# A fused mLSTM-and-experts kernel: a PSUM tile for each bank, another order of the attention step, and the division of the rows moved to GpSimd

## The chip, the cores and the metric

The kernel runs on one core of a Trainium2 chip. The metric is the device time of one execution in microseconds (us), the median of several. The engines are TensorE (PE in the profile; its weight loads are PEld), VectorE (DVE), ScalarE (ACT), GpSimd (POOL) and SyncE (SP), which here only starts transfers; transfers by a list of indices are started by POOL.

## What is computed

An mLSTM (attention with a running matrix state, 4 batches, 8 heads, 768 tokens, head size 40) and behind it a mixture of eight experts, of which each token takes the best one. The attention's rows, 3072 tokens by 320, are the experts' input.

```python
for t in range(S):                                    # attention, per batch and head
    m_new = np.maximum(f_gate[:, :, t] + m, i_gate[:, :, t])
    f_stab, i_stab = np.exp(f_gate[:, :, t] + m - m_new), np.exp(i_gate[:, :, t] - m_new)
    C = f_stab * C + i_stab * outer(v_t, k_t)
    n = f_stab * n + i_stab * k_t
    denom = np.maximum(np.abs(n @ q_t), 1.0)
    y[:, :, t] = sigmoid(o_gate[:, :, t]) * (C @ q_t) / denom
logits = x @ w_gate                                   # x: y as (3072, 320) rows
expert_idx, gate_w = argmax(logits), softmax(logits)[argmax]
for e in range(8):
    mask = expert_idx == e
    out[mask] = gate_w[mask, None] * (np.maximum(x[mask] @ w1[e], 0.0) @ w2[e])
```

## The kernel before

**Attention.** 24 items (128 tokens of one batch, all heads) pass through a pipeline in program order; nothing reorders it, each engine runs its own instructions in the order written. `step(s)` does for item s the `scores` (PE) and `pmul` (DVE, the masked product pp), for item s+1 `weigh` (POOL: qg, kw, cd), for item s-2 `natural` (PE, L322: yT is brought to token-major form in the bank x_ps, with the denominators and the gate logits in further columns) and then, woven together, `state(s-2)` (DVE writes the state cz), `finish(s-2)` (DVE: reciprocal r of the denominators, the divided rows xs at L339, the logits lg), `routing` of a group of items, and some of the long gate operations (`gates`). Then come `choose` when a group of 4 or 2 items is complete (DVE: d, the one-hot oh, running sums ohs), and only behind it, at the step's end, `attend(s-1)` (PE, L290 to L299: the state's and the tokens' products into h_ps) and `gated(s-1)` (DVE, yT). `spread` and `decay` (PE, ACT, POOL) prepare item s+2. `store` writes xs to x_dram in HBM. `scatter` (POOL) writes each token's number to the list of its expert; `place`, `count` and `total` work out its slot with small matmuls (L391 to L393, L431) and DVE operations, the last of them a cast to integer (L413).

**Experts.** `take` loads an expert's list, and `gather` (POOL, L513) fetches J tiles of T rows each by it. `transpose_x` (PE, ACT, DVE) turns them into columns, split into a high part xh and a low part xl; `third(k)` does a third of that. `first` makes eight groups of products with w1 (L546), each group in one of three PSUM banks, and ACT and DVE make the high part hh (L555) and the low part hl (L556) from each. `second` multiplies by w2 (L569) for one tile of tokens at a time, in one of two banks, ACT scales (L573) and POOL scatters y to the output (L574). The heaviest expert, 0, is done in parts "a" (256 tokens, taken early) and "b" (the rest). Expert r+1 is taken at the start of expert r and transposed inside `second` of it. The experts have J x T of 4x128 (three), 4x112, 3x128 (two) and 3x112 (two) rows.

The banks are assigned by these lines; bc_ps and h_ps are one tile of two banks each, and the program tracks a PSUM tile as a whole:

```python
bc_ps = ps1.tile([P, 2, 512], F32, name="bc_ps")
g_ps = ps1.tile([P, 512], F32, name="g_ps")
h_ps = ps1.tile([P, 2, 512], F32, name="h_ps")
bank = [*s_ps, bc_ps[:, 0], bc_ps[:, 1], g_ps, h_ps[:, 0], h_ps[:, 1], x_ps]
turn = {n: itertools.cycle(t) for n, t in (("xt", [*bank[:2], bank[7]]), ("ph", bank[2:5]), ("py", bank[5:7]))}
```

## Time and profile before

| | |
|---|---|
| median of 3 runs | 462.13 us (461.16 to 467.69) |
| the profiled execution | 459.98 us, span of its trace 458.3 us |
| mean granted TensorE clock | 0.907 |
| busy share | PE 80%, DVE 54%, ACT 39%, POOL 35% |
| attention, to the first expert's products | 0 to 182.97 us |
| expert 0, while the other lists are made | 182.97 to 229.87 us |
| experts 1 to 7 | 229.87 to 445.81 us |

A time is the start of an instruction in microseconds from the span's start. Busy time is the time in which an engine worked; idle time is put down to what ended it. The granted clock is the share of full speed that the throttle left to TensorE in a stretch.

### The profile page before, as it was taken

The numbers are of one execution on the slowest core, as the hardware profiler recorded it, in microseconds if no ns is written. First come the engines' busy times: TensorE is split into PE (matmuls) and PEld (weight loads), VectorE is DVE, ScalarE is ACT, GpSimd is POOL, SyncE is SP. The second block draws the span as 40 slices with busy tenths as digits, with TensorE's granted clock in tenths as the row PEclk, the third lists the DMA queues.
The fourth block names the chain that finished last, engine by engine and source line by source line (L and its number), as shares of the span: only waits on it lengthen the run. The fifth ranks groups of instructions, "written<-read, shape, count | busy, mean of one in ns | idle before, by whom it ended". The sixth has DMA issues, their size and how long they took to land. (4 is left out here: it accounts for less than half of the span.)

```text
span 458.3 us, 8799 instructions
## 1 busy us (share of the span) xinstructions
PE 367.6 (80%) x3250; PEld 326.3 (71%) x3250; DVE 248.2 (54%) x587; ACT 179.0 (39%) x429; POOL 162.4 (35%) x198
## 2 busy tenths in 40 slices
PE   7496598786978879679888987988988978889870
PEld 3485487676767768578867875877887868889770
DVE  4779666768698897545335325426515435263200
ACT  4544235354456460145234323424425334353210
POOL 2555258575685653334040240131130140222010
...
GB/s 223 213 264 170 143 119 209 152 187 173 192 245 267 190 50 103 139 81 211 91 91 65 165 105 59 133 119 95 136 122 87 169 130 117 145 126 35 2 20 12
DMA packets 33599, 61.37 MB, mean 134 GB/s; under 512 B 8724, under 2 KB 20253, under 8 KB 33538
## 3 DMA queue, kind: packets, MB, share of 16 engines
...
q14 instruction: 19, 0.16, 0.2%
q10 hardware_dynamic: 192, 0.18, 0.1%
...
## 5 line engine op out<-in xcount | busy, mean ns | idle before, releaser
L225 ACT ACTIVATE dd<-bc_ps,aT 128x128 f32<-128x128 f32 x192 | 52.1, 382 | 84.2 <-PE bc_ps L207 59.5
L574 POOL DMA_INDIRECT out<-y,ls x24 | 23.6, 981 | 160.4 <-ACT y L573 153.4
L569 PE MATMUL h_ps<-w2h,hh 128*128 128x320 f32 (+1 forms) x224 | 72.0, 321 | 8.4 <-ACT y L573 7.2
L569 PE MATMUL h_ps<-w2l,hh 128*128 128x320 f32 (+1 forms) x224 | 69.5, 310 | 0.0
L569 PE MATMUL h_ps<-w2h,hl 128*128 128x320 f32 (+1 forms) x224 | 69.4, 310 | 0.0
L546 PE MATMUL bc_ps<-xh,w1h 128*128 128x512 f32 (+4 forms) x129 | 48.5, 378 | 25.3 <-DVE hl L556 24.0
L556 DVE SCALAR_TENSOR_TENSOR hl<-bc_ps,hh 128x256 fp32r<-128x256 f32 (+4 forms) x48 | 26.5, 552 | 68.4 <-ACT hh L555 67.3
L569 PEld LDWEIGHTS h_ps<-w2h,hh 128*128 128x128 f32 (+1 forms) x224 | 41.3, 184 | 13.2 <-ACT y L573 11.4
L546 PEld LDWEIGHTS bc_ps<-xh,w1h 128*128 128x128 f32 x129 | 25.5, 198 | 33.7 <-DVE hl L556 29.6
L555 ACT ACTIVATE hh<-bc_ps 128x256 fp32r<-128x256 f32 (+4 forms) x48 | 23.4, 489 | 65.9 <-PE bc_ps L546 61.5
L546 PE MATMUL bc_ps<-xh,w1l 128*128 128x512 f32 (+4 forms) x129 | 45.6, 355 | 0.0
L322 PE MATMUL x_ps<-cs,yT 105*128 105x98 f32 x184 | 31.0, 320 | 15.4 <-DVE yT L307 15.4
L271 DVE TENSOR_TENSOR pp<-s_ps,dd 128x512 f32<-128x512 f32 x48 | 31.0, 685 | 21.9 <-PE s_ps L265 13.0
L232 POOL TENSOR_SCALAR_AFFINE_SELECT dd<-dd 128x1024 f32<-128x1024 f32 (+1 forms) x25 | 26.6, 1065 | 42.8 <-ACT dd L225 37.5
L569 PEld LDWEIGHTS h_ps<-w2l,hh 128*128 128x128 f32 (+1 forms) x224 | 41.3, 184 | 0.0
L569 PEld LDWEIGHTS h_ps<-w2h,hl 128*128 128x128 f32 (+1 forms) x224 | 41.3, 184 | 0.0
L322 PEld LDWEIGHTS x_ps<-cs,yT 105*128 105x128 f32 x184 | 26.7, 223 | 19.0 <-DVE yT L307 17.1
L573 ACT ACTIVATE y<-h_ps,ls 128x320 f32<-128x320 f32 (+1 forms) x24 | 12.7, 527 | 68.1 <-issue 55.0
L496 DVE TENSOR_TENSOR w1l<-raw,w1h 128x1024 fp32r<-128x1024 f32 x24 | 31.5, 1315 | 6.6 <-ACT w1h L492 6.6
L295 PE MATMUL h_ps<-pp,tk 128*41 128x128 f32 x368 | 33.2, 337 | 0.9 <-DVE cz L316 0.6
L513 POOL DMA_INDIRECT xg<-x_dram,ls x26 | 27.7, 1066 | 14.5 <-issue 5.5
L496 DVE TENSOR_TENSOR w2l<-raw,w2h 128x640 fp32r<-128x640 f32 x32 | 26.0, 822 | 12.5 <-ACT w2h L492 11.7
...
## 6 DMA issues: line engine op xcount, KB each, us to landing
...
xg<-x_dram,ls POOLq DMA_INDIRECT x26
```

The source lines that it names most:

```text
L225: nc.scalar.activation(dd[:, h, :], bc_ps[:, h // 4, (h % 4) * P : (h % 4 + 1) * P], AF.Exp, bias=aT[:, c, i : i + 1], scale=-1.0,)
L232: nc.gpsimd.affine_select(part, part, pattern=[[0, n], [1, P]], compare_op=ALU.is_ge, fill=0.0, base=0, channel_multiplier=-1)
L271: nc.vector.tensor_mul(pp[:, 4 * k : 4 * k + 4], s_ps[k].rearrange("p (h t) -> p h t", t=P), t["dd"][:, 4 * k : 4 * k + 4])
L295: nc.tensor.matmul(out_of(it, h), v[:, h], t["pp"][:, h], start=c == 0, stop=True, skip_group_check=True)
L322: nc.tensor.matmul(x[:, o], t["yT"][:, o * P : (o + 1) * P], cs[:OR, C_R + o * XW : C_R + (o + 1) * XW], start=True, stop=True,)
L496: nc.vector.tensor_sub(w[name + "l"][:, c], t, f32(w[name + "h"][:, c]))
L513: nc.gpsimd.indirect_dma_start(out=xg[:T, j], out_offset=None, in_=x_dram[: 1 + items * P], in_offset=bass.IndirectOffsetOnAxis(ap=ls[:T, ...
L546: nc.tensor.matmul(ph[:, :n], a[:, k, fs], b[:, k, :n], start=not last and i == 0, stop=last and i == 2)
L555: nc.scalar.activation(hh[:, f, :n], ph[f][:, :n], AF.Relu)
L556: nc.vector.scalar_tensor_tensor(hl[:, f, :n], ph[f][:, :n], 0.0, f32(hh[:, f, :n]), ALU.max, ALU.subtract)
L569: nc.tensor.matmul(py[:T], a[:, f, ts], b[:, f], start=(f == 0 and i == 0), stop=(f == NF - 1 and i == 2))
L574: nc.gpsimd.indirect_dma_start(out=out, out_offset=bass.IndirectOffsetOnAxis(ap=ls[:T, j, 1:2].bitcast(I32), axis=0), in_=y[:T], in_offset ...
```

## The change

- The two banks of bc_ps become two tiles, and `first` takes its banks in the order g, bc1, bc0. The banks of `second` become two tiles of their own, py0 and py1. The transposes of part "a" take the same three banks as the others.
- `attend(s-1)`, `gated(s-1)` and `state(s-1)` stand behind `weigh(s+1)`, ahead of `natural(s-2)`; before, `state` was done a step later and the other two at the step's end.
- Rows are stored undivided, with their eight reciprocals: ACT copies them out of x_ps, DVE writes the reciprocals beside them (328 numbers a row instead of 320), and POOL multiplies the gathered rows by them, a tile at a time, after the J gathers of a take.
- One DVE reduction a group (sums) replaces the running sums, and up to ten small matmuls replace three in `count`, up to eight replace one in `total` (54 more in all). The slot is reduced straight into an integer.
- The long gate operations are issued three a step in steps 2 to 5 (before: four, four and the rest in steps 3 to 5), and the first flip (L175) moves from the end of step 1 into step 2.

```diff
-    bc_ps = ps1.tile([P, 2, 512], F32, name="bc_ps")
+    bc_ps = [ps1.tile([P, 512], F32, name=f"bc_ps{i}") for i in range(2)]
     g_ps = ps1.tile([P, 512], F32, name="g_ps")
-    h_ps = ps1.tile([P, 2, 512], F32, name="h_ps")
     x_ps = ps1.tile([P, 512], F32, name="x_ps")
...
+    turn = {"xt": itertools.cycle([*s_ps, x_ps]), "ph": itertools.cycle([g_ps, bc_ps[1], bc_ps[0]])}
...
+        t["xs"] = xs = sm.tile([P, XR], F32, name=f"xs{it}", tag="xs", bufs=3)
+        nc.scalar.copy(xs[:, :DM].rearrange("p (o w) -> p o w", o=NSLOT), x[:, :, : 2 * D])
...
-        yield nc.vector.reciprocal(r, r)
+        rr = xs[:, DM:].rearrange("p (o j) -> p o j", j=2)
+        yield nc.vector.reciprocal(rr, r)
...
-        for j in range(i0, i0 + n):
-            yield nc.vector.tensor_add(ohs[:, j + 1, :], ohs[:, j, :], oh[:, j, :])
+            yield nc.vector.tensor_reduce(
+                sums[:, group_of(i0)], oh[:, i0 : i0 + n, :].rearrange("p n e -> p e n"), axis=AX.X, op=ALU.add
+            )
...
-        nc.tensor.matmul(pos, ones, ohs[:, i0 : i0 + n], start=False, stop=False)
+        for g in range(group_of(i0)):
+            nc.tensor.matmul(
+                pos, ones, sums[:, g].unsqueeze(1).to_broadcast([P, n, E]), start=False, stop=False,
+                skip_group_check=True,
+            )
+        for j in range(n - 1):
+            nc.tensor.matmul(
+                pos[:, j + 1 :], ones, oh[:, i0 + j].unsqueeze(1).to_broadcast([P, n - 1 - j, E]), start=False,
+                stop=False, skip_group_check=True,
+            )
...
-        ss = sm.tile([P, n], F32, name=f"ss{i0}", tag="ss")
-        yield nc.vector.tensor_reduce(ss, sl, axis=AX.X, op=ALU.add)
-        yield nc.vector.tensor_copy(slot[:, i0 : i0 + n], ss)
+        with nc.allow_low_precision("whole numbers"):
+            yield nc.vector.tensor_reduce(slot[:, i0 : i0 + n], sl, axis=AX.X, op=ALU.add)
...
+        for j in range(J):
+            x = xg[:T, j, :DM].rearrange("p (h d) -> p h d", h=H)
+            nc.gpsimd.tensor_mul(x, x, xg[:T, j, DM:].unsqueeze(2).to_broadcast([T, H, D]))
...
-    BACK = {0: 4, 1: 20, 3: 4, 4: 4, 5: 20}
-    FLIPS = {1: (1, 1), 5: (2, 4)}
+    BACK = {0: 4, 1: 20, 2: 3, 3: 3, 4: 3, 5: 3, 6: 20}
+    FLIPS = {2: (1, 1), 5: (2, 4)}
...
-        if s == NITEM:
+        if ok(s - 1) and s > 1:
             attend(s - 1)
             gated(s - 1)
+            state(s - 1)
...
-        if ok(s - 1) and 1 < s < NITEM:
-            attend(s - 1)
-            gated(s - 1)
...
+        ps3 = ctx.enter_context(tc.tile_pool(name="ps3", bufs=1, space=PS))
+        turn["py"] = itertools.cycle([ps3.tile([P, 512], F32, name=f"py{i}") for i in range(2)])
```

TensorE in step 13 of the attention, before: behind the scores of item 13 comes natural of item 11, then attend of item 12 (its qg and pp).

```order
L265 MATMUL s_ps_121<-tq_1090 128x128
L322 MATMUL x_ps<-cs,yT_1345 128x98 x4
L290 MATMUL h_ps<-qg_1210,cz_116 41x128 x8
L295 MATMUL h_ps<-pp_1298,tk_986 41x128 x8
L299 MATMUL h_ps<-tk_986,kw_1212 40x41 x8
```

The same step after:

```order
L265 MATMUL s_ps_121<-tq_1088 128x128
L289 MATMUL h_ps<-qg_1209,cz_116 41x128 x8
L294 MATMUL h_ps<-pp_1297,tk_987 41x128 x8
L298 MATMUL h_ps<-tk_987,kw_1211 40x41 x8
L323 MATMUL x_ps<-cs,yT_1330 128x98 x4
```

The three lines of attend have moved ahead of natural.

VectorE in step 13, which completes a group of four items, before: state, finish, choose (mx to ohs), and then yT.

```order
L314 TENSOR_TENSOR cz_119<-cd_1111,h_ps 104x164
L333 TENSOR_SCALAR r_1403<-x_ps 128x8
L334 TENSOR_TENSOR r_1403<-r_1403,x_ps 128x8
L335 RECIPROCAL r_1403<-r_1403 128x8
L339 TENSOR_TENSOR xs_1407<-x_ps,r_1403 128x320
L348 TENSOR_TENSOR pl_1409<-x_ps,r_1403 128x64
L352 TENSOR_REDUCE lg<-pl_1409 128x8
L368 TENSOR_REDUCE mx_1412<-lg 128x4
L370 TENSOR_TENSOR d_1414<-lg,mx_1412 128x32
L374 SCALAR_TENSOR_TENSOR sc_1416<-d_1414,cs 128x32
L378 TENSOR_REDUCE m_1418<-sc_1416 128x4
L379 TENSOR_TENSOR oh<-sc_1416,m_1418 128x32
```

Behind these stand the four sums `ohs` (L381) and then yT of item 12 (L307). The same step after:

```order
L306 SCALAR_TENSOR_TENSOR yT_1421<-og_1092,h_ps 105x512
L315 TENSOR_TENSOR cz_116<-cd_1213,h_ps 104x164
L336 TENSOR_SCALAR r_1430<-x_ps 128x8
L337 TENSOR_TENSOR r_1430<-r_1430,x_ps 128x8
L339 RECIPROCAL xs_1428<-r_1430 128x8
L341 TENSOR_TENSOR pl_1434<-x_ps,xs_1428 128x64
L345 TENSOR_REDUCE lg<-pl_1434 128x8
L362 TENSOR_REDUCE mx_1437<-lg 128x4
L364 TENSOR_TENSOR d_1439<-lg,mx_1437 128x32
L368 SCALAR_TENSOR_TENSOR sc_1441<-d_1439,cs 128x32
L372 TENSOR_REDUCE m_1443<-sc_1441 128x4
L373 TENSOR_TENSOR oh<-sc_1441,m_1443 128x32
```

yT and the state now come ahead of finish and choose; the product xs is gone, and one reduction (sums) follows instead of four.

GpSimd at expert 0 and 1, before: the last scatter to the lists, the gathers of part b, those of expert 1, the output of expert 0 (ya, yb) and the gathers of expert 2.

```order
L420 DMA lst<-rec,slot 28672x3
L513 DMA xgb<-x_dram,lsb 128x320 x2
L513 DMA xg_2681<-x_dram,ls_2679 128x320 x4
L574 DMA out<-ya_2774,ls_99 3072x320
L574 DMA out<-ya_2817,ls_99 3072x320
L574 DMA out<-yb_2952,lsb 3072x320
L574 DMA out<-yb_2981,lsb 3072x320
L513 DMA xg_2990<-x_dram,ls_2988 128x320 x4
```

The same place after:

```order
L424 DMA lst<-rec,slot 28672x3
L519 DMA xgb<-x_dram,lsb 128x328 x2
L525 TENSOR_TENSOR xgb<-xgb 128x320 x2
L519 DMA xg_2709<-x_dram,ls_2707 128x328 x4
L525 TENSOR_TENSOR xg_2709<-xg_2709 128x320 x4
L583 DMA out<-ya_2806,ls_99 3072x320
L583 DMA out<-ya_2849,ls_99 3072x320
L583 DMA out<-yb_2984,lsb 3072x320
L583 DMA out<-yb_3013,lsb 3072x320
L519 DMA xg_3022<-x_dram,ls_3020 128x328 x4
L525 TENSOR_TENSOR xg_3022<-xg_3022 128x320 x4
```

Each take's products follow its gathers on the same queue: the gathers of expert 1 stand behind the two products of part b.

## Rows read from the trace of the kernel before

**Rows 1.** Busy time in five stretches of the span. Columns: stretch, its length, busy time of PE, PEld, DVE, ACT, POOL (with their instructions), granted clock, DMA share, GB/s. The stretches are steps 2 to 5, 6 to 13 and 14 to 22 of the attention, expert 0, and experts 1 to 7.

```profile
20.57:55.31 34.74, 24.18 (x293) 21.46 (x292) 26.43 (x64) 12.48 (x40) 14.82 (x15) 0.79 0.71 206
55.31:107.59 52.28, 45.12 (x680) 39.65 (x679) 35.56 (x102) 25.49 (x83) 34.17 (x44) 0.86 0.65 165
107.59:171.74 64.15, 51.74 (x729) 44.52 (x727) 55.60 (x159) 34.69 (x102) 40.92 (x54) 0.84 0.77 185
...
182.97:229.87 46.90, 37.81 (x249) 35.63 (x246) 21.60 (x57) 16.07 (x35) 13.81 (x16) 0.89 0.47 129
229.87:445.81 215.94, 186.42 (x1087) 168.46 (x1085) 87.49 (x141) 80.05 (x140) 44.22 (x44) 0.99 0.35 102
```

**Rows 2.** The waits of the whole span. Columns: engine, tile and line that waited, what ended the wait, us in total, times, longest.

```profile
PE bc_ps L546 <- DVE hl L556: 28.4, 19, 2.8
...
PE x_ps L322 <- DVE yT L307: 15.4, 8, 3.7
```

**Rows 3.** TensorE's groups of instructions in experts 1 to 7. Columns: line, operation, tiles, shapes, count, busy us, mean ns, idle us before them and what ended it.

```profile
L569 PE MATMUL h_ps<-w2h,hh 128*128 128x320 f32 (+1 forms) x192 | 61.5, 320 | 7.2 <-ACT y L573 7.2
...
L546 PE MATMUL bc_ps<-xh,w1h 128*128 128x512 f32 (+3 forms) x111 | 41.8, 377 | 22.3 <-DVE hl L556 21.0 <-DVE used L589 1.4
...
L546 PE MATMUL g_ps<-xh,w1h 128*128 128x336 f32 (+3 forms) x57 | 20.1, 354 | 0.0
```

**Rows 4.** TensorE in time, products of expert 2. Columns: start, us, engine, line, operation, tiles, shapes, count, idle before and releaser.

```profile
274.24 0.39 PE L546 MATMUL bc_ps<-xh,w1h 128*128 128x512 f32 x1
274.47 0.39 PE L546 MATMUL bc_ps<-xh,w1l 128*128 128x512 f32 x1
276.89 0.51 PE L546 MATMUL bc_ps<-xh,w1h 128*128 128x512 f32 x1 [2.03 <-DVE hl L556]
277.23 0.40 PE L546 MATMUL bc_ps<-xh,w1l 128*128 128x512 f32 x1
```

**Rows 5.** TensorE in time, a step of the attention that completes no group, from scores to scores.

```profile
96.36 1.16 PE L265 MATMUL s_ps<-tq 40*128 40x128 f32 x16
...
99.29 0.67 PE L290 MATMUL h_ps<-qg,cz 40*41 40x128 f32 x16 [0.71 <-DVE r L333]
...
101.97 1.16 PE L265 MATMUL s_ps<-tq 40*128 40x128 f32 x16
```

**Rows 6.** VectorE in time at the end of step 13, which completes a group.

```profile
106.48 2.02 DVE L370 TENSOR_TENSOR d<-lg,mx 128x32 f32<-128x32 f32 x1
...
110.94 0.69 DVE L307 SCALAR_TENSOR_TENSOR yT<-og,h_ps 105x512 f32<-105x512 f32 x1
```

**Rows 7.** TensorE in time behind that step.

```profile
111.68 2.03 PE L322 MATMUL x_ps<-cs,yT 105*128 105x98 f32 x8 [2.93 <-DVE yT L307]
```

**Rows 8.** TensorE in time, the first flip.

```profile
19.36 0.31 PE L175 MATMUL h_ps<-cs,a_sb 32*128 32x32 f32 x1 [5.35 <-DVE a_sb L164]
```

**Rows 9.** Two stretches of 20 us, columns as in Rows 1.

```profile
120.00:140.00 20.00, 15.87 (x249) 13.74 (x249) 17.35 (x41) 12.16 (x35) 15.28 (x19) 0.91 1.04 277
140.00:160.00 20.00, 17.29 (x256) 15.02 (x257) 17.84 (x55) 9.69 (x29) 13.76 (x20) 0.83 0.92 227
```

**Rows 10.** Costs of five kinds of instructions, columns as in Rows 3.

```profile
L247 POOL TENSOR_TENSOR kw<-tk,dd 128x320 f32<-128x320 f32 x20 | 15.3, 766 | 12.5 <-issue 11.5 <-POOL qg L244 0.8
...
L573 ACT ACTIVATE y<-h_ps,ls 128x320 f32<-128x320 f32 (+1 forms) x24 | 12.7, 527 | 68.1 <-issue 55.0 <-PE h_ps L569 9.2 <-PEq L888 3.9
...
L339 DVE TENSOR_TENSOR xs<-x_ps,r 128x320 f32<-128x320 f32 x23 | 11.2, 488 | 0.5
...
L381 DVE TENSOR_TENSOR ohs<-ohs,oh 128x8 bf16<-128x8 bf16 x24 | 6.5, 271 | 0.8
L413 DVE CAST slot<-ss 128x4 int32<-128x4 f32 (+1 forms) x8 | 5.5, 691 | 0.1
```

**Rows 11.** GpSimd in time, expert 0: the last scatter to the lists, the gathers of part b, the last gather of expert 1.

```profile
192.95 0.95 POOL L420 DMA_INDIRECT lst<-rec,slot  x1 [0.21 <-issue]
199.77 0.98 POOL L513 DMA_INDIRECT xgb<-x_dram,lsb  x1 [5.87 <-DMA lsb<-lst]
201.06 0.96 POOL L513 DMA_INDIRECT xgb<-x_dram,lsb  x1 [0.30 <-issue]
...
208.72 0.95 POOL L513 DMA_INDIRECT xg<-x_dram,ls  x1 [0.30 <-issue]
```

**Rows 12.** TensorE in time, the first transposes of expert 1's tiles, the last of them behind a wait for its tile.

```profile
212.31 0.73 PE L531 MATMUL s_ps<-cs,xg 128*128 128x128 f32 x3
213.46 0.33 PE L531 MATMUL s_ps<-cs,xg 128*128 128x128 f32 x1 [0.41 <-DMA xg<-x_dram,ls]
```

**Rows 13.** TensorE in time, the first product of the sixth expert in order (3x128 rows).

```profile
365.99 0.34 PE L546 MATMUL bc_ps<-xh,w1h 128*128 128x384 f32 x1
```

**Rows 14.** GpSimd in time, two first gathers: for expert 2, at the start of expert 1, and for the expert behind the sixth (3x112 rows).

```profile
232.21 0.99 POOL L513 DMA_INDIRECT xg<-x_dram,ls  x1 [0.31 <-PE bc_ps L546]
...
370.92 0.96 POOL L513 DMA_INDIRECT xg<-x_dram,ls  x1 [2.90 <-PE bc_ps L546]
```

**Rows 15.** VectorE and GpSimd in time, steps 16 and 17 of the attention.

```profile
124.36 0.46 POOL L254 TENSOR_TENSOR cd<-cz,gb 104x164 f32<-104x164 f32 x1
...
127.78 3.41 DVE L496 TENSOR_TENSOR w1l<-raw,w1h 128x1024 fp32r<-128x1024 f32 x1
...
129.97 1.54 POOL L254 TENSOR_TENSOR cd<-cz,gb 104x164 f32<-104x164 f32 x1
```

More of the change, by code (lines that the diff above doesn't have):

```diff
@@ L123, in mlstm_moe_kernel @@
     s_ps = [ps1.tile([P, 512], F32, name=f"s_ps{i}") for i in range(2)]
-    bc_ps = ps1.tile([P, 2, 512], F32, name="bc_ps")
+    bc_ps = [ps1.tile([P, 512], F32, name=f"bc_ps{i}") for i in range(2)]
     g_ps = ps1.tile([P, 512], F32, name="g_ps")
-    h_ps = ps1.tile([P, 2, 512], F32, name="h_ps")
     x_ps = ps1.tile([P, 512], F32, name="x_ps")
-    bank = [*s_ps, bc_ps[:, 0], bc_ps[:, 1], g_ps, h_ps[:, 0], h_ps[:, 1], x_ps]
-    turn = {n: itertools.cycle(t) for n, t in (("xt", [*bank[:2], bank[7]]), ("ph", bank[2:5]), ("py", bank[5:7]))}
+    h_ps = p1.enter_context(tc.tile_pool(name="ps2", bufs=1, space=PS)).tile([P, 2, 512], F32, name="h_ps")
+    turn = {"xt": itertools.cycle([*s_ps, x_ps]), "ph": itertools.cycle([g_ps, bc_ps[1], bc_ps[0]])}
     u_ps = h_ps[:KR, 0, 2 * P : 2 * P + NSLOT * OW].rearrange("p (o w) -> p o w", w=OW)
@@ L273, in pmul @@
             )
-    hT_of = lambda it: h_ps if it < NITEM - 1 else bc_ps
-    x_of = lambda it: x_ps if it < NITEM - 1 else h_ps[:, 0]
+    x_of = lambda it: x_ps if it < NITEM - 1 else bc_ps[0]
     def out_of(it, h):
         o, r = (h // 2) % 2, HR * (h % 2)
-        return hT_of(it)[r : r + OW, h // 4, o * P : (o + 1) * P]
+        return h_ps[r : r + OW, h // 4, o * P : (o + 1) * P]
     def attend(it):
@@ L325, in natural, with finish @@
             )
-    def finish(it, late=False):
+    def finish(it):
         t = st[it]
         x = t["x"]
+        t["xs"] = xs = sm.tile([P, XR], F32, name=f"xs{it}", tag="xs", bufs=3)
+        nc.scalar.copy(xs[:, :DM].rearrange("p (o w) -> p o w", o=NSLOT), x[:, :, : 2 * D])
         r = sm.tile([P, NSLOT, 2], F32, name=f"r{it}", tag="r")
@@ L334, in finish @@
         yield nc.vector.tensor_tensor(r, r, nq, ALU.max)
-        yield nc.vector.reciprocal(r, r)
-        t["xs"] = xs = sm.tile([P, DM], F32, name=f"xs{it}", tag="xs", bufs=3)
-        def rows():
-            return nc.vector.tensor_mul(
-                xs.rearrange("p (o j d) -> p o j d", o=NSLOT, j=2),
-                x[:, :, : 2 * D].rearrange("p o (j d) -> p o j d", j=2),
-                r.unsqueeze(3).to_broadcast([P, NSLOT, 2, D]),
-            )
-        if not late:
-            yield rows()
+        rr = xs[:, DM:].rearrange("p (o j) -> p o j", j=2)
+        yield nc.vector.reciprocal(rr, r)
         pl = sm.tile([P, NSLOT, 2, E], F32, name=f"pl{it}", tag="pl")
@@ L361, in mlstm_moe_kernel @@
     rt = {}
+    starts = [i0 for i0, _ in GROUPS.values()]
+    group_of = starts.index
     def choose(i0, n):
@@ L379, in choose @@
         yield nc.vector.tensor_tensor(oh[:, i0 : i0 + n, :], sc, b8(m2), ALU.is_equal)
-        for j in range(i0, i0 + n):
-            yield nc.vector.tensor_add(ohs[:, j + 1, :], ohs[:, j, :], oh[:, j, :])
+        with nc.allow_low_precision("counts of at most four"):
+            yield nc.vector.tensor_reduce(
+                sums[:, group_of(i0)], oh[:, i0 : i0 + n, :].rearrange("p n e -> p e n"), axis=AX.X, op=ALU.add
+            )
     def weights_of(i0, n):
@@ L430, in total @@
         rt["pc", items] = pc = pos_ps[:, 4 * E : 5 * E]
-        nc.tensor.matmul(pc, ones, ohs[:, items], start=True, stop=True)
+        n = sum(i0 < items for i0 in starts)
+        for g in range(n):
+            nc.tensor.matmul(pc, ones, sums[:, g], start=g == 0, stop=g == n - 1)
     def rank(k, items):
@@ L528, in third @@
             r = min(P, DM - k * P)
-            pt = bank[(0, 1, 6)[k]] if key == "a" else next(turn["xt"])
+            pt = next(turn["xt"])
             for j in range(J):
@@ L634, in stir @@
         for _ in range(n):
-            nc.tensor.matmul(bank[0], busy[:, :P], busy, start=True, stop=True)
+            nc.tensor.matmul(s_ps[0], busy[:, :P], busy, start=True, stop=True)
     def start():
@@ L680, in start @@
         gated(0)
+        state(0)
         for b in range(B):
@@ L724, in step @@
             pmul(s)
+        if s in FLIPS:
+            flip(*FLIPS[s])
         if s in SPLITS:
@@ L740, in step @@
         weave(
-            state(s - 2) if ok(s - 2) and (s - 2) // B < NCH - 1 else None,
             finish(s - 2) if ok(s - 2) else None,
@@ L745, in step @@
         )
-        if s - 2 in GROUPS and s < NITEM - 1:
+        if s - 2 in GROUPS and s < NITEM:
             weave(choose(*GROUPS[s - 2]))
@@ L754, in step @@
             third(1)
-        if ok(s - 1) and 1 < s < NITEM:
-            attend(s - 1)
-            gated(s - 1)
-        if s in FLIPS:
-            flip(*FLIPS[s])
-        if s - 2 in GROUPS and s == NITEM - 1:
-            weave(choose(*GROUPS[s - 2]))
         if todo and s >= EARLY and s != EARLY + 4:
@@ L812, in mlstm_moe_kernel @@
         store(NITEM - 2)
-        weave(finish(NITEM - 1, late=True))
+        weave(finish(NITEM - 1))
         weave(choose(NITEM - 2, 2))
```

39 lines of the change are left out of this document (20 added, 19 removed).

## The prediction, made before the changed kernel was timed

> **What bounds the kernel now.** I read the table of stretches first [rows 1], since the limits differ by stage. In experts 1 to 7 TensorE is busy 186.4 of 215.9 us at a clock of 0.99, and nothing else comes near. In steps 6 to 13 of the attention it is busy 45.1 of 52.3, but at 0.86. In steps 2 to 5 VectorE is the fullest (26.4 of 34.7, TensorE 24.2 at 0.79). In steps 14 to 22 the transfers come up: 1.04 and 0.92 of the DMA engines' time between 120 and 160 us [rows 9].
>
> Then the waits [rows 2]. TensorE's largest one, 28.4 us, is that of the experts' products for the low part hl; the next, 15.4, is natural's wait for yT. The groups of the experts [rows 3] say where the first sits: 22.3 us ahead of products into bc_ps, nothing ahead of those into g_ps. Both have the same readers. So it is not the readers' speed but the tile of two banks: a group for the second bank of bc_ps waits for the readers of its first bank, which TensorE has only just left, while g_ps had two groups' time. The timeline shows one such wait, 2.03 us [rows 4]. The products of `second` wait 7.2 for the same reason on h_ps.
>
> In the attention a plain step takes 5.61 us, 0.71 of it idle ahead of L290 [rows 5]; back to back it is 4.90. When a group completes, VectorE does `choose` first, 2.02 for d among it, and yT only at 110.94 [rows 6]; natural starts 2.93 late [rows 7].
>
> **The change, part by part.** The sum is made against the profiled execution, 459.98 us.
>
> *Banks in experts 1 to 7.* With own tiles in the order g, bc1, bc0 a group waits for the readers of three groups back, as g_ps does now, and g_ps shows no wait. What goes with a wait is a little more than its idle time: from 274.47 to 277.23 are 2.76 us for two products that take 0.23 each, 2.30 lost for 2.03 idle [rows 4], a factor of 1.13. The idle time is 22.3 + 7.2 = 29.5; the 1.4 put to `used` (another matter, the leftovers' arithmetic) I leave. 28.1 x 1.13 = 31.8 back. What is late next is TensorE itself: 0.99 of its clock, ACT and VectorE 80 and 87 us of 216 [rows 1].
>
> *Division on POOL, experts.* Not in the trace: a POOL product of 128x320 with a broadcast operand in place. Nearest row: kw, the same engine and size, 0.77 us [rows 10]; below it VectorE's own product, 0.49 [rows 10]; above it, cd beside VectorE's subtraction took 1.54 where a plain one takes 0.46 [rows 15], which on kw's scale would be 2.5. I take 0.77. It can't be below nothing, since POOL did none of it. A tile is ready when gathered, landed and multiplied. Gathers follow each other at 1.29 [rows 11]; the last one of expert 1 ended its issue at 209.67 and its tile let TensorE on at 213.46 [rows 11, 12], 3.8 later. Three tiles: 2 x 1.29 + 0.95 + 3.8 + 0.77 = 8.1 from the first gather; four: 9.4. TensorE wants them when `first` ends: 64 products of 0.23 [rows 4] at 512 columns are 14.8 us and in proportion 12.9 at 448, 11.1 at 384, 9.7 at 336. Most gathers start some 2.3 us into an expert (229.87 [rows 1] to 232.21 [rows 14]): 10.4 to 11.7, in time. But in the sixth the first gather starts at 370.92, 4.9 behind its first product [rows 13, 14]: 13.0 against 11.1, 1.9 lost; the seventh likewise, 13.0 against 9.7, 3.3 lost. Together 5.2 against the gain. Experts 1 to 7: 31.8 - 5.2 = **27 less**.
>
> Here the trace can be set beside a rule. POOL's kw takes 766 ns against 488 for VectorE's product of the same size [rows 10], 1.57 times. The Trainium skill, GPSIMD Engine Reference, section 4.1 (Engine selection), says to leave elementwise products of two inputs to VectorE, GpSimd being about twice as slow, which speaks against this move. By it a product would be 0.98, an estimate from that page, and the time some 2 us longer than my sum; by the row it is 0.77.
>
> *Expert 0, 182.97 to 229.87.* The bank waits go here too, so part "a" comes through sooner, but part "b" can't: its rows depend on the last items' routing. Before, the last scatter starts 10.0 us behind the stage's start (192.95) and part b's gather 6.8 later [rows 11]. Shorter routing (no cast of 0.69, no product of 0.49 [rows 10]) brings that to about 8.9 and 15.7. Two gathers, 1.29 + 0.96, landing 3.8 and two products, 1.54: part b is ready at 23.3. The gathers of expert 1 are queued behind these products on POOL: four of them at 1.29, landing and the last product end at 23.3 + 3.9 + 0.95 + 3.8 + 0.77 = 32.7. TensorE comes to the transposes of expert 1 well before, since they stand only two groups into part b. From those transposes to expert 1 it needed 17.6 before (212.31 [rows 12] to 229.87), 17.2 without the waits. 32.7 + 17.2 = 49.9 against 46.9: **3 more**. All that the banks give here is spent on the queue. If the products cost nothing it is 5 less; at 2.5 each, 9 more than this.
>
> *Steps 6 to 13.* attend, gated and state ahead of natural: the waits of L290 (put to r; what it needs is the state cz, just ahead on VectorE) and of natural for yT go, as cz and yT are then a whole step old. `choose` delays only what comes behind. Floor 4.90 a step [rows 5]; VectorE has 35.56 / 8 = 4.4 [rows 1], and loses 0.49 for xs and some of the sums (0.27 each [rows 10]). New: ACT's copy, by its like (y, 0.53 [rows 10]), stands behind decay's exponentials, and VectorE's finish waits for it, as both read the whole tile x_ps; behind finish on VectorE are choose and the next masked products. I allow 0.45 a step for that and for half clock: 5.35 x 8 = 42.8, **9.5 less**. The matmuls of the sums (54 in all, tiny) lie inside it. If VectorE's waits cost nothing it is 4.95 a step, 12.7 less.
>
> *Steps 2 to 5.* VectorE-bound: 26.43 - 4 x 0.49 - 0.75 (three sums of 0.27 fewer, nearly) = 23.7, 5.9 a step; 0.4 for the wait on ACT makes 6.3, 25.2 against 34.7, 9.5 less. The gates, even over four steps, are within that. The flip in step 2 lets the scores pass, of its 5.35 [rows 8] I count 1.1, as the gate operations ahead of it stay. **10.6 less**.
>
> *Steps 14 to 22.* Between 120 and 160 the transfers moved 20 x 277 + 20 x 227, at 277 GB/s 36.4 us of the 40 [rows 9]: 3.6 to be had there, the rest of the 64 us holds natural's 2.93 [rows 7] and its like, less what the lower clock (0.84 [rows 1]) takes back: **6 less**. The row of 328 numbers adds 2.5% to the stores. Steps 23 and 24 gain a wait or two and lose the two products of part a's tiles: nil.
>
> Sum: -27 + 3 - 9.5 - 10.6 - 6 = -50.1, 409.9; the median stands to the profiled execution as 462.13 to 459.98, so **411 us**.
>
> **Rivals.**
>
> *The attention hardly gains.* The copy on ACT comes behind decay, VectorE waits, transfers bind anyway. For it: VectorE's and ACT's order, the DMA share; against it: steps 6 to 13 have no transfer limit (0.65 [rows 1]). Attention 10 less, not 26: **428**.
>
> *Everything is hidden.* Products beside landings, steps at 4.95. Attention 31 less, expert 0 5 less, experts 32 less: 392, as a median **394**. Against it: the queue on POOL at part b.
>
> *The change doesn't do what it says*: the three-bank turn doesn't take the waits away, since hl is late by its own chain (ACT behind the weights' conversion). Experts nil instead of 27 less: **439**. Against it: g_ps's empty idle column [rows 3].
>
> *Slower: POOL's products are dear.* They run while VectorE subtracts the weights' parts, and the trace shows cd at 1.54 beside a w1l of 3.41 [rows 15]. At a price p above about 2 the products, not the landings, end a take: four tiles at 4.8 + 4p from the first gather, three at 4.8 + 3p. At p = 4: 20.8 and 16.8; with gathers 2.3 behind the start, 23.1 against 14.8 twice, 19.1 against 12.9, 19.1 against 11.1, then 21.7 against 11.1 and 9.7: 53 lost instead of 5.2; expert 0 gets some 18 more, part a's two tiles 6.5. 409.9 + 72 = 482, as a median **484**. It decides from p = 3.2, where all the gain is gone. Against it: kw runs beside the same subtractions at 766 on average. The Trainium skill, SBUF — State Buffer, section Who interferes with whom, has the rule behind this: VectorE and GpSimd share a pair of ports by an exclusive lock, the second fully blocks. The trace agrees at the one place just named (1.54 for 0.46), and no row shows it for a product like this.
>
> **How the numbers follow.** Forecast 0.52; attention hardly gains 0.20; all hidden 0.14; banks don't help 0.07; dear products 0.07, of it 0.04 above 2% and 0.02 within it. The forecast's own spread, from the terms' bounds: 400 to 421. The range reaches from below the all-hidden case to above the small-attention case, and takes in most of a product of 2.5: 387 to 433, which leaves out some 0.16. A measurement of this kernel tells 2% from no change. Faster by more: 0.93; within: 0.03; slower: 0.04.
>
> **What would show it.** Bank steps: no wait of L546 for hl in experts, TensorE's share there above 0.95. Order: L290 and natural without waits, plain steps near 5.3. POOL: products near 0.77; one wait of the transposes at expert 1 (some 6 us) and two, of 2 to 3 us, near the end. Expert 0 near 50 us. The prediction is wrong if products take over 2, if VectorE's finish waits over half a microsecond a step for ACT's copy, or if ACT's hh becomes what the products wait for.

## The result and the profile after

The changed kernel takes 396.18 us (median of 4 executions, 392.04 to 401.09) against 462.75 before. The ratio is 0.848, 95% interval 0.836 to 0.859; executions in which the granted clock was lower throughout are left out of it, which is why it stands a little below the quotient of the medians. A second series of the same kernel gave 390.89 and 0.844 (0.840 to 0.848). Forecast were 411 (its own sum gives 411.8), in a range of 387 to 433.

The profiled execution took 392.04, its span is 390.0 us. Busy time of each engine on its page:

```profile
PE 347.3 (89%) x3304; PEld 318.3 (82%) x3304; DVE 226.1 (58%) x539; ACT 188.3 (48%) x453; POOL 188.2 (48%) x225
```

The stretches that answer to [rows 1], columns as there; the fourth is steps 23 and 24, and the last two are expert 0 and experts 1 to 7:

```profile
18.25:47.74 29.49, 23.72 (x293) 21.41 (x293) 20.12 (x53) 11.75 (x36) 14.31 (x16) 0.74 0.75 204
47.74:87.58 39.84, 38.76 (x686) 34.70 (x684) 31.98 (x98) 28.39 (x91) 33.25 (x44) 1.00 0.88 221
87.58:138.93 51.35, 46.81 (x758) 41.32 (x756) 41.76 (x131) 36.89 (x108) 43.17 (x53) 0.93 0.97 248
138.93:152.85 13.92, 12.10 (x119) 9.81 (x120) 10.01 (x45) 3.18 (x8) 6.66 (x10) 0.75 0.39 120
152.85:195.64 42.79, 35.98 (x255) 34.63 (x253) 20.30 (x50) 16.29 (x35) 17.96 (x22) 0.92 0.48 134
195.64:377.76 182.12, 178.52 (x1094) 169.76 (x1092) 90.99 (x141) 80.15 (x140) 62.92 (x64) 0.99 0.42 121
```

Experts 1 to 7 lost 33.8 us of their 215.9, expert 0 lost 4.1, steps 14 to 22 lost 12.8, steps 6 to 13 lost 12.4, steps 2 to 5 with what lies before them 7.6; steps 23 and 24 take 2.7 longer. A second trace of the same kernel (span 391.3 us) has 42.73, 51.80, 12.45, 41.30 and 183.55 us for the last five of these stretches: two traces of one kernel differ by up to 2.9 us in a stretch, and the comparisons of single traces below can show no less. In steps 6 to 13 the reader should look at two columns at once: the idle time fell from 7.2 to 1.1, and TensorE's own busy time from 45.1 to 38.8, with the granted clock up from 0.86 to 1.00 (41.7 at 0.92 in the second trace).

TensorE's groups in experts 1 to 7 (columns as in [rows 3]): the column of idle time is empty where it held 7.2 and 22.3, and what is left are transposes that wait for the rows.

```profile
L578 PE MATMUL py<-w2h,hh 128*128 128x320 f32 (+1 forms) x192 | 61.4, 320 | 0.0
...
L555 PE MATMUL bc_ps<-xh,w1h 128*128 128x512 f32 (+3 forms) x114 | 40.0, 352 | 0.0
...
L540 PE MATMUL s_ps<-cs,xg 128*128 128x128 f32 (+1 forms) x40 | 7.1, 276 | 3.6 <-POOL xg L525 2.7 <-DMA xg<-x_dram,ls 0.9
```

TensorE in time, a plain step (it answers to [rows 5]): 4.73 from scores to scores, attend ahead of natural, no idle entry.

```profile
92.56 1.16 PE L265 MATMUL s_ps<-tq 40*128 40x128 f32 x16
93.65 0.66 PE L289 MATMUL h_ps<-qg,cz 40*41 40x128 f32 x16
...
95.55 1.13 PE L323 MATMUL x_ps<-cs,yT 105*128 105x98 f32 x8
...
97.29 1.16 PE L265 MATMUL s_ps<-tq 40*128 40x128 f32 x16
```

TensorE's waits in the whole span. Those of [rows 2] are gone; new are those for POOL's products (xgb, xg), for the flip (aT), and of the scores for the masked products of the step before.

```profile
PE s_ps L265 <- DVE pp L271: 6.2, 3, 2.8
PE s_ps L540 <- POOL xgb L525: 4.5, 2, 2.2
PE s_ps L540 <- POOL xg L525: 4.4, 7, 1.3
PE h_ps L289 <- DVE aT L178: 3.0, 1, 3.0
```

Among VectorE's waits is one that the prediction gave as a sign of being wrong, finish (r) waiting for ACT's copy (xs): 15.9 us over 24 steps, 0.66 a step, where it allowed half a microsecond.

```profile
DVE r L336 <- ACT xs L333: 15.9, 15, 3.3
```

GpSimd in time at expert 0 (it answers to [rows 11]). The gathers of expert 1 do stand behind part b's second product, as forecast; the four products then end at 181.84.

```profile
167.14 0.98 POOL L519 DMA_INDIRECT xgb<-x_dram,lsb  x1 [5.80 <-DMA lsb<-lst]
...
172.80 0.72 POOL L525 TENSOR_TENSOR xgb<-xgb 128x320 f32<-128x320 f32 x1 [1.86 <-DMA xgb<-x_dram,lsb]
173.67 0.99 POOL L519 DMA_INDIRECT xg<-x_dram,ls  x1
...
178.44 3.40 POOL L525 TENSOR_TENSOR xg<-xg 128x320 f32<-128x320 f32 x4
```

### The profile page after: what moved, and what is told of

Same layout as the page of the kernel before. It is cut to its first block, busy times and chain, and to the rows that moved or that the text cites. A ratio compares the mean times of both kernels' runs of the same rounds, so it can differ in the third digit from the quotient of the medians.

```text
span 390.0 us, 8965 instructions
## 1 busy us (share of the span) xinstructions
PE 347.3 (89%) x3304; PEld 318.3 (82%) x3304; DVE 226.1 (58%) x539; ACT 188.3 (48%) x453; POOL 188.2 (48%) x225
## 4 chain that ended last, share of the span: by engine, by line
PE 50%; DMA 19%; issue 10%; DVE 9%; POOL 5%; ACT 3%; SPq 1%; POOLq 0%; ACTq 0%; another core or an unknown queue 0%; DVEq 0%
PE py L578 17%; PE bc_ps L555 12%; PE g_ps L555 6%; DMA x_dram<-xs 5%; DMA og<-in_og 5%; PE s_ps L265 3%; DMA out<-y,ls 3%; PE x_ps L323 3%; PE h_ps L294 3%; POOL xg L519 2%; DVE pp L271 2%; POOL xg L525 2%; PE h_ps L289 2%; DMA cs<-in_cst 1%; ACT dd L225 1%
## 5 line engine op out<-in xcount | busy, mean ns | idle before, releaser
L578 PE MATMUL py<-w2h,hh 128*128 128x320 f32 (+1 forms) x224 | 71.8, 320 | 0.0
L578 PE MATMUL py<-w2l,hh 128*128 128x320 f32 (+1 forms) x224 | 70.0, 312 | 0.0
L578 PE MATMUL py<-w2h,hl 128*128 128x320 f32 (+1 forms) x224 | 70.0, 312 | 0.0
L565 DVE SCALAR_TENSOR_TENSOR hl<-bc_ps,hh 128x512 fp32r<-128x512 f32 (+4 forms) x48 | 26.4, 551 | 37.2 <-ACT hh L564 32.8
L555 PE MATMUL bc_ps<-xh,w1h 128*128 128x512 f32 (+4 forms) x129 | 44.4, 347 | 0.0
L555 PE MATMUL bc_ps<-xh,w1l 128*128 128x512 f32 (+4 forms) x129 | 44.2, 346 | 0.0
L578 PEld LDWEIGHTS py<-w2h,hh 128*128 128x128 f32 (+1 forms) x224 | 41.9, 187 | 0.0
L578 PEld LDWEIGHTS py<-w2l,hh 128*128 128x128 f32 (+1 forms) x224 | 41.8, 187 | 0.0
L578 PEld LDWEIGHTS py<-w2h,hl 128*128 128x128 f32 (+1 forms) x224 | 41.7, 186 | 0.0
L265 PE MATMUL s_ps<-tq 40*128 40x128 f32 x384 | 33.0, 303 | 6.4 <-DVE pp L271 6.2
L265 PEld LDWEIGHTS s_ps<-tq 40*128 40x128 f32 x384 | 27.3, 202 | 9.8 <-DVE pp L271 7.5
L424 POOL DMA_INDIRECT lst<-rec,slot x24 | 26.0, 1082 | 12.3 <-DVE slot L417 7.3
```

The costliest lines, as they stand in the source:

```text
L265: nc.tensor.matmul(s_ps[h // 4][:, p * P : (p + 1) * P], k, q, start=True, stop=True)
L424: ins = nc.gpsimd.indirect_dma_start(out=lst, out_offset=bass.IndirectOffsetOnAxis(ap=slot[:, it : it + 1], axis=0), in_=rec[:, it, :], in ...
L555: nc.tensor.matmul(ph[:, :n], a[:, k, fs], b[:, k, :n], start=not last and i == 0, stop=last and i == 2)
L565: nc.vector.scalar_tensor_tensor(hl[:, f, :n], ph[f][:, :n], 0.0, f32(hh[:, f, :n]), ALU.max, ALU.subtract)
L578: nc.tensor.matmul(py[:T], a[:, f, ts], b[:, f], start=(f == 0 and i == 0), stop=(f == NF - 1 and i == 2))
```

## The experiments

Each time is a median of its own executions, with the ratio to the kernel before on the same chip; stretches are read from the profiled execution.

**Banks alone, on the kernel before.** bc_ps, py and the order of the banks as after, nothing else (the last item's products and projection then also lie in the tiles that the change gives them).

```diff
-    bc_ps = ps1.tile([P, 2, 512], F32, name="bc_ps")
+    bc_ps = [ps1.tile([P, 512], F32, name=f"bc_ps{i}") for i in range(2)]
...
+    turn = {"xt": itertools.cycle([*s_ps, x_ps]), "ph": itertools.cycle([g_ps, bc_ps[1], bc_ps[0]])}
...
+        turn["py"] = itertools.cycle([ps3.tile([P, 512], F32, name=f"py{i}") for i in range(2)])
```

> The kernel before with the PSUM tiles of the change alone (bc0, bc1, py0, py1 and the order g, bc1, bc0); everything else as before. Theory (the tile of two banks makes TensorE wait, nothing else does): the attention stays at 183 us, experts 1 to 7 go from 215.9 to 174 to 178 us without any wait of the products for hl or of second for y, expert 0 from 46.9 to 43 to 46, since part b's rows come no sooner; the time is 415 to 423. Rival (the readers are late anyway, or the gain needs the other parts): experts 1 to 7 above 195 us, the time above 438.

Measured 422.92 us, 0.913 (0.903 to 0.922). Its stretches, the attention, expert 0 and experts 1 to 7:

```profile
0.00:185.28 185.28, 152.23 (x1920) 128.87 (x1921) 134.09 (x393) 82.89 (x254) 104.11 (x137) 0.80 0.72 185
185.28:226.46 41.18, 35.20 (x248) 33.61 (x246) 20.79 (x54) 15.83 (x35) 12.83 (x16) 0.92 0.37 118
226.46:403.87 177.41, 175.93 (x1087) 168.07 (x1085) 86.89 (x141) 79.98 (x140) 43.10 (x44) 1.00 0.42 124
```

The attention didn't gain, experts 1 to 7 gave 38.5 and expert 0 gave 5.7. The order of the three banks was changed with their tiles and was not tried alone. But the trace of before shows which reader ended the wait of [rows 4], at 276.89: that of the group just left, and not that of the group three back, which had ended at 272.56.

```profile
271.87 0.69 DVE L556 SCALAR_TENSOR_TENSOR hl<-bc_ps,hh 128x512 fp32r<-128x512 f32 x1 [2.78 <-ACT hh L555]
...
276.16 0.67 DVE L556 SCALAR_TENSOR_TENSOR hl<-bc_ps,hh 128x512 fp32r<-128x512 f32 x1
```

So the tile of two banks was the cause of the experts' waits, and the banks alone carry over half of the change (8.7% of some 15.4%).

**attend, gated and state back at the step's end**, the rest as after.

```diff
-        if ok(s - 1) and s > 1:
+        if s == NITEM:
             attend(s - 1)
             gated(s - 1)
-            state(s - 1)
-        if s == NITEM:
             third(0)
...
+        if ok(s - 1) and 1 < s < NITEM:
+            attend(s - 1)
+            gated(s - 1)
+            state(s - 1)
```

> The changed kernel with attend, gated and state of item s-1 back at the end of the step, behind natural, finish and choose. Theory (the order takes the waits out of the attention): natural waits for yT again where a group completes, some 3 us each in six steps, and the clock behind each wait is lower; steps 6 to 22 take 8 to 18 us longer, the time is 401 to 412. Rival (VectorE's shorter work did it, not the order): 2 us or less, the time is 392 to 396, and no wait of natural above 1 us.

Measured 407.55 us, 0.878 (0.872 to 0.884). Steps 6 to 13 and 14 to 22, and the wait that came back:

```profile
47.70:90.60 42.90, 40.56 (x684) 35.84 (x683) 29.90 (x92) 27.74 (x88) 33.17 (x44) 0.96 0.81 208
90.60:153.20 62.60, 55.27 (x758) 47.95 (x756) 46.12 (x140) 38.31 (x111) 41.70 (x54) 0.79 0.76 195
```

```profile
PE x_ps L323 <- DVE yT L306: 9.5, 7, 2.1
```

These steps are 14.3 us longer than in the trace above, and 11.0 longer than in the second trace of the changed kernel. Of the 14.3, TensorE's idle time takes 4.1 and its busy time 10.3. In steps 14 to 22 the same work keeps it busy for 55.3 instead of 46.8, at 0.79 instead of 0.93: the lower clock costs more than the waits. That the waits lower it is argued from their standing together; no run here changes the one without the other.

**Division on VectorE again**, a product out of PSUM in finish; no copy on ACT, no products on POOL.

```diff
-        nc.scalar.copy(xs[:, :DM].rearrange("p (o w) -> p o w", o=NSLOT), x[:, :, : 2 * D])
...
+        yield nc.vector.tensor_mul(
+            xs[:, :DM].rearrange("p (o j d) -> p o j d", o=NSLOT, j=2),
+            x[:, :, : 2 * D].rearrange("p o (j d) -> p o j d", j=2),
+            rr.unsqueeze(3).to_broadcast([P, NSLOT, 2, D]),
+        )
...
-            nc.gpsimd.tensor_mul(x, x, xg[:T, j, DM:].unsqueeze(2).to_broadcast([T, H, D]))
```

> The changed kernel with the division back on VectorE as a product out of PSUM in finish, no copy on ACT and no products on POOL; rows of 328 numbers are still stored and gathered. Theory (the products cost the waits of the transposes, the division on VectorE is hidden behind TensorE): expert 0 gives back 6 to 9 us of its waits for xgb and xg1, the late experts 2 to 4, the attention loses 0 to 3; the time is 381 to 389. Rival (VectorE, 0.49 us a step longer, becomes the attention's bound): steps 2 to 22 take 6 to 10 us longer, the time is 391 to 397.

Measured 389.78 us, 0.837 (0.830 to 0.843), which overlaps the changed kernel's intervals. Steps 14 to 22, expert 0, experts 1 to 7, and its waits:

```profile
86.50:141.20 54.70, 51.26 (x759) 44.66 (x757) 50.29 (x139) 35.28 (x102) 44.10 (x54) 0.85 0.88 234
...
154.68:196.48 41.80, 35.38 (x254) 34.44 (x253) 20.30 (x51) 15.66 (x34) 13.52 (x16) 0.92 0.45 135
196.48:377.08 180.60, 178.23 (x1094) 169.91 (x1092) 87.22 (x141) 80.16 (x140) 44.80 (x44) 0.99 0.42 122
```

```profile
PE s_ps L541 <- DMA xgb<-x_dram,lsb: 5.8, 2, 3.4
```

Expert 0 gave back 1.0, not 6 to 9: without the products TensorE waits for the rows themselves (5.8 for xgb, where the products' wait was 4.5). The late experts gave back 1.5, not 2 to 4. Steps 14 to 22 took 3.4 more (2.9 against the second trace). The theory's gain and the rival's loss are both small: the move of the division can't be told from no change.

**Products three times over.** Each gathered row is divided three times instead of once; the rest of the work stays.

```diff
-            nc.gpsimd.tensor_mul(x, x, xg[:T, j, DM:].unsqueeze(2).to_broadcast([T, H, D]))
+            for _ in range(3):
+                nc.gpsimd.tensor_mul(x, x, xg[:T, j, DM:].unsqueeze(2).to_broadcast([T, H, D]))
```

> The changed kernel with each product of gathered rows on POOL done three times in a row, so that a tile costs some 2.4 us instead of 0.8; the rows are divided three times over. Theory (the price of a product decides as in the forecast's slower case): expert 0 takes some 9 us longer, steps 23 and 24 some 3, experts 1 to 7 some 17; the time is 415 to 427. Rival (landings hide the products): below 404.

Measured 439.40 us, 0.949 (0.944 to 0.955). Expert 0, experts 1 to 7, the cost of a product (78 of them, 0.90 each), and the wait:

```profile
152.66:204.63 51.97, 38.96 (x254) 37.41 (x253) 20.16 (x48) 16.61 (x36) 26.62 (x34) 0.81 0.36 101
204.63:420.98 216.35, 189.35 (x1094) 178.75 (x1092) 94.13 (x141) 80.58 (x140) 99.99 (x104) 0.93 0.34 102
```

```profile
L526 POOL TENSOR_TENSOR xg<-xg 128x320 f32<-128x320 f32 (+1 forms) x78 | 69.4, 899 | 5.7 <-DMA xg<-x_dram,ls 1.2 <-issue 0.3
```

```profile
PE s_ps L541 <- POOL xg L526: 34.5, 17, 3.4
```

This is outside the 415 to 427 expected. At 2.7 a tile, where 2.4 was expected, the products do end the takes. Expert 0 took the 9 expected, steps 23 and 24 took 13.3 us against 13.9, where some 3 more were expected, experts 1 to 7 34 instead of 17. The forecast's formula, which counts waits alone, gives some 22 more at 2.7, and TensorE's idle time there rose by 23.4; the other 10.8 are busy time, at a clock of 0.93. So the slower case of the forecast was real in kind, and larger than its formula by what the clock took. The price at which all of the gain is gone was not tried: at 2.7 the kernel is still 5% faster than before.

**Lists of experts 2 to 7 loaded behind that of expert 1.**

```diff
+        def listed(key, row, J, T):
+            lists[key] = ls = xp.tile([P, 4, 3], F32, name=f"ls{key}", tag="ls", bufs=9)
+            load_list(ls, row, J, T)
...
                 xs[1] = take(1, es[1] * SS, *CAPS[1])
+                for r in range(2, E):
+                    listed(r, es[r] * SS, *CAPS[r])
```

> The changed kernel, the lists of experts 2 to 7 loaded right behind the list of expert 1, instead of each at the start of the expert before it. Theory (the two waits of the late experts come from the list's load, which stands on SP's queue behind weight loads that wait for their buffers, and not from the price of the products): the gathers start 2 to 3 us into an expert, the transposes wait under 0.5 us in all experts, experts 1 to 7 take 175 to 178 us instead of 182; the time is 386 to 391. Rival (products and landing make the wait wherever the gather starts): experts 1 to 7 stay at 181 to 183.

Measured 387.89 us, 0.845 (0.837 to 0.852), which can't be told from the changed kernel's 0.844 to 0.848; the effect is read from the traces. In the changed kernel the list's load stands on SP's queue behind eight weight loads. It goes out 1.0 us behind the sixth expert's start at 307.14 (0.4 to 0.6 ahead of the start in the experts before), and the first gather waits for it:

```profile
291.54 16.20 SPq L493 DMA_DIRECT2D raw<-in_w  x8
308.14 0.34 SPq L512 DMA_DIRECT2D ls<-lst  x1
```

```profile
312.57 0.97 POOL L519 DMA_INDIRECT xg<-x_dram,ls  x1 [3.39 <-DMA ls<-lst]
```

With the lists early (expert's start 305.62), the same gather, and the stretch of experts 1 to 7:

```profile
307.96 0.97 POOL L519 DMA_INDIRECT xg<-x_dram,ls  x1 [0.30 <-issue]
```

```profile
194.15:370.20 176.05, 176.05 (x1094) 168.38 (x1092) 89.29 (x141) 80.05 (x140) 62.73 (x64) 1.00 0.44 126
```

TensorE is busy without a gap, with all products in place. So the late experts' waits (6.1 us in all, 7.5 against the second trace) came from the late list and not from the price of a product. The place on the queue is part of that lateness; the load also took 4.4 us from its issue to the gather, where the experts before have at most 3.1 to 4.0, and the two were not separated.

**Division on VectorE and early lists together**, the two diffs above.

> The kernel with the division on VectorE and, besides, the lists of experts 2 to 7 loaded early. Theory (the two gains are apart): experts 1 to 7 at 175 to 177 us, the rest as with the division on VectorE alone; the time is 382 to 388. Rival (the products cost nothing once the lists come early): the same time as with early lists alone, within 2 us.

Its four executions took 384.3, 390.0, 392.8 and 475.6 us; no interval is to be had from them. Experts 1 to 7 took 176.1 in the trace, as with the lists alone, which agrees with both, and steps 14 to 22 took 55.1, as with the division on VectorE alone; the total stays inconclusive between theory and rival.

**Gates and flips as before.**

```diff
-    BACK = {0: 4, 1: 20, 2: 3, 3: 3, 4: 3, 5: 3, 6: 20}
-    FLIPS = {2: (1, 1), 5: (2, 4)}
+    BACK = {0: 4, 1: 20, 3: 4, 4: 4, 5: 20}
+    FLIPS = {1: (1, 1), 5: (2, 4)}
...
-        if s in FLIPS:
-            flip(*FLIPS[s])
...
+        if s in FLIPS:
+            flip(*FLIPS[s])
```

The change moved both flips, that of step 5 from the step's end to its middle; here both stand at the end of their step again.

> The changed kernel with the long gate operations issued as before (four, four and the rest in steps 3 to 5) and both flips at the ends of steps 1 and 5. Theory (VectorE bounds steps 2 to 5, and the flip keeps the scores waiting): step 6 starts 3 to 8 us later than 47.7, the rest is unchanged, the time is 396 to 402. Rival (order and division gave all of it): within 2 us of the changed kernel.

Measured 392.55 us, 0.855 (0.847 to 0.862). Step 6 starts at 48.2 (scores of item 0 0.8 earlier, so 1.3 later than after), step 7 at 58.0 against 53.8, and expert 1 at 195.4 against 195.6. The theory fell as to the time; a few microseconds in steps 2 to 6 are visible and don't reach the end of expert 0.

**Running sums and the slot's cast as before**, and then the sums alone.

```diff
-            yield nc.vector.tensor_reduce(
-                sums[:, group_of(i0)], oh[:, i0 : i0 + n, :].rearrange("p n e -> p e n"), axis=AX.X, op=ALU.add
-            )
+        for j in range(i0, i0 + n):
+            yield nc.vector.tensor_add(ohs[:, j + 1, :], ohs[:, j, :], oh[:, j, :])
...
```

> The changed kernel with the running sums on VectorE and the slot's cast as before, and three small matmuls a group instead of up to ten. Theory (the sums are a small matter, 0.27 us each on VectorE where it waits for nothing else): steps 6 to 22 take 0 to 4 us longer, 1 to 2 us more from the last item's routing to part b; the time is 393 to 399. Rival (54 matmuls more on TensorE, which bounds the steps, cost more than they save): the time is 388 to 392.

> The changed kernel with the running sums on VectorE and three small matmuls as before, but the slot still reduced straight into an integer. Theory (the chain of dependent sums, 1.7 to 2.5 us a group, is what TensorE's small matmuls wait for): most of the 11 us that sums and cast cost together, the time is 399 to 404. Rival (the cast of 0.7 us, on the way to the slot, does it): the time is 392 to 396.

Measured 404.14 us, 0.881 (0.873 to 0.888), with both; 403.64 us, 0.875 (0.870 to 0.880), with the sums and no cast. So the sums are worth some 9 to 13 us (the trace's span is 400.1 against 390.0 and 391.3, the median 403.64 against 390.89), and the cast can't be told from nothing. With the sums alone steps 6 to 22 took 101.4 us, against 91.2 and 94.5 in the two traces of the changed kernel. VectorE with running sums (and the cast), then in the changed kernel, at the same group; and TensorE's wait in the middle of the step:

```profile
95.06 2.45 DVE L375 TENSOR_TENSOR ohs<-ohs,oh 128x8 bf16<-128x8 bf16 x4
```

```profile
90.80 0.21 DVE L375 TENSOR_REDUCE sums<-oh 128x8 bf16<-128x32 bf16 x1
```

```profile
97.56 0.17 PE L425 MATMUL x_ps<-ohs,ones 128*128 128x8 bf16 x1 [1.52 <-DVE ohs L375]
```

Four dependent additions take 2.45 for 0.21, and the small matmul that needs their end stands on TensorE ahead of the next spread and scores, which wait with it. Their number is the smaller part of it. An addition takes 0.16 in the median; the last of these four took 1.86 and ended 0.03 behind a product of GpSimd:

```profile
95.65 1.86 DVE L375 TENSOR_TENSOR ohs<-ohs,oh 128x8 bf16<-128x8 bf16 x1
96.21 1.27 POOL L244 TENSOR_TENSOR qg<-tq,gb 104x512 f32<-104x512 f32 x1
```

The group before it shows the same (1.86, with qg). That GpSimd's work holds the addition is read from these ends; no run moves qg away from it.

**Flips behind attend.**

```diff
-        if s in FLIPS:
-            flip(*FLIPS[s])
...
             state(s - 1)
+        if s in FLIPS:
+            flip(*FLIPS[s])
```

> The changed kernel with the two flips of steps 2 and 5 behind attend, gated and state of those steps instead of ahead of them. Theory (the change puts the flip ahead of attend, and attend's products into the same tile wait for VectorE to read the flip, 1.6 and 3.0 us, with a lower clock behind): steps 2 and 5 get shorter, step 7 starts 4 to 8 us earlier counted from the first scores, the time is 387 to 392. Rival (VectorE has the same work, so the wait moves to the next product): 2 us or less.

Measured 392.80 us, 0.845 (0.839 to 0.851). In the changed kernel attend waits for the flip's reader; here the flip waits for the state, which lies in the same tile h_ps:

```profile
41.62 1.11 PE L289 MATMUL h_ps<-qg,cz 40*41 40x128 f32 x16 [2.96 <-DVE aT L178]
```

```profile
42.95 0.43 PE L175 MATMUL h_ps<-cs,a_sb 32*128 32x32 f32 x4 [1.69 <-DVE cz L315]
...
46.38 2.08 PE L265 MATMUL s_ps<-tq 40*128 40x128 f32 x16
```

The rival holds: the wait moves, and the scores of step 6 run at 2.08 instead of 1.16, at a granted clock of 0.50, the lower level (1.2 GHz).

**A version with three of these**: early lists, flips behind attend, part b's products on VectorE just ahead of its transposes. To the diffs above it adds

```diff
             if j == HT - 1:
+                divide(nc.vector, xs["b"][1], 4 - HT, P)
                 for k in range(3):
```

where `divide` is the loop of products, which `gather` no longer runs for part b.

> The changed kernel with the lists of experts 2 to 7 loaded early, the flips behind attend, and part b's two products on VectorE just ahead of its transposes, so that the gathers of expert 1 follow those of part b on POOL. Theory (the gains are apart): 6 to 7 us from the lists, 3 to 6 from the flips, 2 to 4 from part b; the time is 376 to 384. Rival (what is gained ahead of part b is lost waiting for its rows): 384 to 389.

> The changed kernel once more, unedited, beside the others on the same chip: 390 to 398.

Measured 387.84 us, 0.836 (0.831 to 0.841), beside 0.844 (0.840 to 0.848) for the changed kernel in the same series: a per cent less, the intervals just touching. It is not in the 376 to 384 of the theory but in the rival's 384 to 389. Expert 0 took 43.4 us, no less than 42.8, so part b's products on VectorE gave nothing, and experts 1 to 7 took 176.2, as with early lists alone, whose median (387.89) is the same. Of the three only the lists hold. The 377.88 of the profiled execution is the shortest time measured here; the other five are 383.97 to 393.28.

## Why the prediction was right, step by step

The direction and the range held. The forecast of 411 was 15 to 20 us too slow and its own spread, 400 to 421, was missed; the range held because it had been drawn around the rivals. The time came out where the rival "everything is hidden" stood (394), to which a chance of 0.14 was given, and by its terms: experts 32 less (33.8 measured), expert 0 5 less (4.1), the attention 31 less (30.1). Of the mechanisms those of the banks and of the order held; expert 0, the sums and ACT's copy were wrong.

*Banks.* Right in kind: the empty idle column of g_ps in [rows 3] did tell how three turns would go. Mis-sized: 31.8 were counted, 38.5 measured with the banks alone (39.9 between the kernel before and early lists). TensorE's waits in experts 1 to 7, before:

```profile
PE bc_ps L546 <- DVE hl L556: 21.0, 15, 2.0
PE h_ps L569 <- ACT y L573: 7.2, 17, 0.7
PE bc_ps L546 <- DVE used L589: 1.4, 1, 1.4
```

The 1.4 that the sum left out as another matter went too: nothing is left ahead of L555. And the factor of 1.13 was made from one long wait [rows 4], which lost 0.27 us beyond its 2.03 of idle time. Taken as a price of each wait and not as a factor, the same row gives 29.5 + 33 x 0.27 = 38.4.

*POOL's products.* A product was taken at 0.77 from kw's row; it took 0.92 on average (23.9 us for 26), but hardly one took that. Of all 28, 22 took 0.71 to 0.74, and six 1.36 to 1.78. Each of the six began while VectorE subtracted the weights' parts (w1l or w2l) and ended some 0.58 behind that subtraction, as here:

```profile
203.01 1.64 DVE L502 TENSOR_TENSOR w1l<-raw,w1h 128x1024 fp32r<-128x1024 f32 x1 [0.24 <-ACT w1h L498]
203.46 1.77 POOL L525 TENSOR_TENSOR xg<-xg 128x320 f32<-128x320 f32 x1
```

So the row was right for a product that stands alone, and the hold that the prediction had seen at cd [rows 15] and put into a rival is real for products like these, at six places. The Trainium skill, GPSIMD Engine Reference, section 4.1 (Engine selection), has GpSimd about twice as slow as VectorE for such products, and by it the prediction estimated 0.98. The measurement says 0.73 in the median against 0.49 for VectorE's product (L339 in the version with the division there), 1.5 times. The Trainium skill's advice there, to leave such products to VectorE, made no difference that could be measured here. The 5.2 us of late gathers were right in size (6.1) and in place, but the cause is the late list.

*Expert 0.* This step failed: 3 more forecast, 4.1 less measured (5.6 in the second trace). The queue on POOL was as described, and TensorE waited there (4.5 and 2.3), but the wait for the landing stands in its place without it. The sum put the last product at 32.7 behind the stage's start; it ended at 29.0. The last scatter came 7.5 behind the start, not 8.9, and the four products ran straight behind the last gather, their first rows landed by then, where the sum had a landing of 3.8 ahead of the last. From there to expert 1 it took 13.8 us instead of 17.2: the 17.2 were counted from the first of expert 1's transposes and set behind the last, which stood 1.15 later [rows 12], and part b's own bank waits were counted at 0.4, where the trace of before holds 2.2 us of idle time behind 213.5. Nor do the 5 less of the rival follow from these terms: without products they give 26.9 + 17.2 = 44.1, 2.8 less.

*Steps 6 to 22.* 15.5 less forecast, 25.2 measured, 21.9 in the second trace. Four terms failed. The sums were called small, 0.27 each, and are worth 9 to 13: the mean of one operation [rows 10] shows neither that single ones are held for 1.86 nor that TensorE waits for the last of a chain of four. The allowance of 0.45 a step was made for ACT's copy and the lower clock. VectorE did wait for the copy, but this wait hardly reaches TensorE, whose idle time in steps 6 to 13 is 1.1 and 1.0 in the two traces; they took 4.98 and 5.34 a step, at 1.00 and 0.92 of the clock. And the lower clock was put down as something that takes gains back, where nearly half of the gain is busy time at a higher clock: TensorE's fell by 6.4 in steps 6 to 13 and 4.9 in steps 14 to 22 (3.4 and 3.9 in the second trace). The 36.4 us for the transfers between 120 and 160 were no floor: they now run through all of steps 14 to 22, at 248 GB/s (185 before) and a DMA share of 0.97; whether they bind now was not tried.

*Steps 2 to 5*: 10.6 forecast, 7.6 measured. The flip in the middle of a step makes attend wait 2.96, which wasn't seen; the two experiments on flips and gates show no place for it that is better by more than can be measured.

*Steps 23 and 24*: nil forecast, 2.7 more measured, 1.2 in the second trace. The two products of part a are not the reason: with products three times over these steps took 13.3 us, without them 13.5, and 13.9 here. Nor is the clock, 0.75 for 0.69 before. 1.6 of it is idle time, most of that one wait of part a's transposes in x_ps for VectorE's routing (1.5, sl at L414), the bank that the change gave them; the rest is open.
